# Dense 64-row chunks for the first stage of a maxout network, repacked by DMA, so that both products run as concurrent 64-row TensorE tiles

## Chip, cores, metric

One NeuronCore of a Trainium2 chip. The metric is the device time of the kernel in microseconds, median of several runs.

## The reference, cut to what matters

```python
# x (8, 4160, 192); weight (8 heads, 7 taps)
w = softmax(weight, axis=-1)
y[b, s, h, g] = sum_k w[h, k] * x_pad[b, s + k, h, g]      # causal, head = 24 channels
h = maximum(maximum(y @ w1, y @ w2), y @ w3)               # 192 -> 768
out = h @ w_out                                            # 768 -> 192, 33280 rows, fp32
```

The kernels use max(a, b, c) = max(a-c, b-c, 0) + c: the first stage computes y(w1-w3) and y(w2-w3), a relu and a maximum, and the second stage adds yM with M = w3 w_out.

## The kernel before

Rows come in 65 blocks of 512. The convolution is a matmul with a band matrix, one 32-column tile per head, so a head of 24 channels lies in a slot of 32 PSUM rows, and 192 channels take two halves of 128 rows.

```python
for (wsrc, q) in ...:                                   # weights padded the same way (cut)
    for half in range(2):
        for (s0, c0, cnt) in slot_rows(half):           # 24 rows each
            q.dma_start(out=st[s0:s0 + cnt, half, :], in_=wsrc[c0:c0 + cnt, :])

def conv(t):                                            # 40 matmuls, four column tiles at once
    ...
    for i in range(2):
        nc.scalar.copy(out=y[:, i, 0:N], in_=G[i][:, 0:N])

def l1(t, j):                                           # one 128-column group of the 768
    for i in range(2):                                  # the two products
        for half in range(2):
            nc.tensor.matmul(ps[i], lhsT=wd[i][:, half, P*j:P*(j+1)], rhs=y[:, half, :],
                             start=(half == 0), stop=(half == 1))
    nc.scalar.activation(out=r, in_=ps[0], func=AF.Relu)
    nc.vector.tensor_max(out=hs[t][:, j, :], in0=r, in1=ps[1])

for t in range(NB + 1):                                 # cut
    load_x(t + 3); cast_x(t + 2)                        # SyncE queue; GpSimd
    l1(t, 0); conv(t + 1); l1(t, 1)
    for j in range(2, NJ): st2(t - 1, j - 2); l1(t, j)
    store(t - 1)                                        # SyncE queue
```

## Time and profile before

| | before |
|---|---|
| time, median of 4 runs | 598.8 us |
| TensorE / VectorE / ScalarE / GpSimd busy | 94 / 57 / 50 / 12% |
| share of TensorE in the chain that ended last | 94% |
| one block | 8.50 us |
| mean granted TensorE clock | 0.997 |

The chain of work that ended last is the view to start from. It follows, back from the last instruction, what released each step. Where one engine holds nearly all of it, only shorter work on that engine helps; where it changes hands in a fixed pattern, the pattern is a loop, and its terms can be added up. The lines are in the prediction.

### The profile page before, as it was taken

How to read it: one execution, taken by the hardware profiler on the slowest of the kernel's cores; microseconds unless marked ns; L12 is line 12 of the kernel's file. 1: busy time of each engine (PE TensorE's matmuls, PEld its weight loads, DVE VectorE, ACT ScalarE, POOL GpSimd, SP SyncE). 2: the span in 40 equal slices, each digit the busy share in tenths (PEclk: the TensorE clock that was granted, in tenths of full speed). 3: DMA queues.
4: the chain of work that ended last, by engine and by line, in shares of the span. 5: the costliest groups of instructions: out<-in, count | busy, mean ns of one | idle time of the engine just before them, and what ended most of it. 6: DMA issues, size and time to landing. Idle time of an engine off the chain costs nothing.

```text
span 597.4 us, 15039 instructions
## 1 busy us (share of the span) xinstructions
PE 562.2 (94%) x6300; PEld 361.1 (60%) x6300; DVE 342.9 (57%) x542; ACT 299.2 (50%) x523; POOL 72.0 (12%) x95
## 2 busy tenths in 40 slices
PE   0199999999999999999999999999999999999995
PEld 0066666666666666666666666666666666666663
DVE  1645656555655565556555656565555656565663
ACT  1135555555555555555555555555555555555551
POOL 2200111101111011101101111011101110111100
PEclk9999999999999999999999999999999999999998
DMA  7502432333234323442344334323443343324211
GB/s 206 172 1 61 119 109 83 109 120 112 83 105 120 114 87 100 121 118 83 98 121 120 86 94 120 120 87 92 121 121 89 91 119 112 103 86 118 83 55 53
DMA packets 79107, 61.40 MB, mean 103 GB/s; under 512 B 2912, under 2 KB 78208, under 8 KB 79040
## 3 DMA queue, kind: packets, MB, share of 16 engines
q1 hardware_dynamic: 78032, 58.43, 33.3%
q10 hardware_dynamic: 1008, 2.02, 1.0%
q8 instruction: 49, 0.80, 0.6%
q14 instruction: 18, 0.15, 0.1%
HBM read 34.34 MB, written 26.09 MB: 101 GB/s over the span
## 4 chain that ended last, share of the span: by engine, by line
PE 94%; DMA 3%; DVE 1%; ACT 1%; ACTq 0%; issue 0%; SPq 0%
PE l L238 58%; PE pso L256 22%; PE pso L253 7%; PE G L221 6%; DMA xf<-in_x_dram 1%; PE pm L204 1%; DMA ws<-in_moe_w_dram 1%; DMA wk<-in_weight_dram 1%; DMA Rd<-R 1%; ACTq L170 0%; DVE h L242 0%; DVE ws L167 0%; ACT r L241 0%; ACT wo L189 0%; SPq L116 0%
## 5 line engine op out<-in xcount | busy, mean ns | idle before, releaser
L238 PE MATMUL l<-y,wd 128*128 128x512 f16 x1560 | 392.4, 381 | 9.0 <-ACT y L228 9.0
L242 DVE TENSOR_TENSOR h<-r,l 128x512 f16<-128x512 f16 x390 | 268.2, 688 | 224.8 <-ACT r L241 220.4
L241 ACT ACTIVATE r<-l 128x512 f16<-128x512 f32 x390 | 234.1, 600 | 235.2 <-PE l L238 235.2
L238 PEld LDWEIGHTS <-wd 128*128 128x128 f16 x1560 | 143.8, 98 | 121.2 <-DVE wd L186 9.6
L256 PE MATMUL pso<-wo,h 128*128 128x192 f16 x1560 | 171.4, 246 | 0.4 <-DVE h L242 0.4
L256 PEld LDWEIGHTS <-h 128*128 128x128 f16 x1560 | 132.7, 98 | 0.6 <-DVE h L242 0.6
L127 POOL CAST x<-xf 128x960 f16<-128x960 f32 (+3 forms) x88 | 70.0, 800 | 487.3 <-DMA xf<-in_x_dram 358.0
L253 PEld LDWEIGHTS <-y 128*128 128x128 f16 x520 | 50.8, 98 | 60.7
L253 PE MATMUL pso<-m,y 128*128 128x192 f16 x520 | 85.4, 246 | 0.0
L228 ACT CAST y<-G 128x512 f16<-128x512 f32 x130 | 69.8, 589 | 28.0 <-PE G L221 28.0
L259 DVE COPY o<-pso 128x384 f32<-128x384 f32 x130 | 71.6, 551 | 1.8 <-PE pso L256 1.8
L221 PEld LDWEIGHTS <-x 128*32 128x32 f16 (+2 forms) x2624 | 36.6, 98 | 45.5 <-issue 40.0
L221 PE MATMUL G<-band,x 128*32 128x122 f16 (+3 forms) x2624 | 43.1, 211 | 18.4 <-DVE band L154 18.4
L189 ACT CAST wo<-wos 128x1152 f16<-128x1152 f32 x1 | 1.2, 1152 | 21.6 <-DMA ws<-in_moe_w_dram 21.6
L154 DVE COPY band<-bandc 128x1072 f16<-128x1072 f16 x1 | 2.5, 2530 | 9.5 <-DMA bandc<-Rd 9.5
L186 DVE TENSOR_TENSOR wd<-ws,ws 128x768 f16<-128x768 f32 x4 | 3.8, 959 | 4.2 <-DMA ws<-in_moe_w_dram 4.2
L204 PE MATMUL pm<-wos,w3t 128*128 128x192 f32 x24 | 4.2, 330 | 0.0
L204 PEld LDWEIGHTS pm<-wos,w3t 128*128 128x128 f32 x24 | 3.9, 190 | 0.2 <-DVE w3t L199 0.2
L167 DVE MEMSET ws<- 128x1536 f32 x2 | 2.7, 1338 | 0.5 <-issue 0.3
L206 DVE CAST m<-pm 128x192 f16<-128x192 f32 x2 | 0.7, 357 | 3.1 <-PE pm L204 3.1
L198 PE MATMUL pt<-ident,ws 128*128 128x128 f32 x12 | 1.7, 277 | 0.7 <-DVE w3t L199 0.7
L141 DVE TENSOR_REDUCE wsum<-wexp 128x8 f32<-128x56 f32 x1 | 0.3, 251 | 3.2 <-ACT wexp L139 3.2
(14 smaller groups left out, 8.9 us busy)
## 6 DMA issues: line engine op xcount, KB each, us to landing
out_dram<-o SPq DMA_DIRECT2D x64, 384.0 KB
xf<-in_x_dram SPq DMA_DIRECT2D x48, 480.0 KB
xf<-in_x_dram SPq DMA_DIRECT2D x16, 384.0 KB
ws<-in_moe_w_dram ACTq DMA_DIRECT2D x16, 72.0 KB
xf<-in_x_dram SPq DMA_DIRECT2D x8, 96.0 KB
ws<-in_moe_w_dram SPq DMA_DIRECT2D x8, 72.0 KB
wos<-in_moe_w_out_dram SPq DMA_DIRECT2D x1, 576.0 KB
xf<-in_x_dram SPq DMA_DIRECT2D x8, 70.5 KB
```

Of the source, the lines that this page charges most:

```text
L127: nc.gpsimd.tensor_copy(out=x16[0:rl, q0:q1, :], in_=xf[0:rl, q0:q1, :])
L167: eng.memset(st[:], 0.0)
L186: nc.vector.tensor_sub(out=d16[:, half, :], in0=wa[:, half, :], in1=w3s[:, half, :])
L204: nc.tensor.matmul(ps[:], lhsT=w3t[:, j, half, :], rhs=wos[:, j, :], start=(j == 0), stop=(j == NJ - 1))
L221: nc.tensor.matmul(G[h // 4][32 * g:32 * g + 32, lo:hi], lhsT=x16[0:rlen, q, cb:cb + 32], rhs=band[0:rlen, h, cc:cc + hi - lo], start=True ...
L228: nc.scalar.copy(out=y[:, i, 0:N], in_=G[i][:, 0:N])
L238: nc.tensor.matmul(ps[i][:, 0:N], lhsT=wd[i][:, half, P * j:P * (j + 1)], rhs=y[:, half, 0:N], start=(half == 0), stop=(half == 1))
L241: nc.scalar.activation(out=r[:, 0:N], in_=ps[0][:, 0:N], func=AF.Relu)
L242: nc.vector.tensor_max(out=hs[t][:, j, 0:N], in0=r[:, 0:N], in1=ps[1][:, 0:N])
L253: nc.tensor.matmul(ps[:, s % 2, :], lhsT=y[:, half, sl], rhs=m16[:, half, :], start=(half == 0), stop=False)
L256: nc.tensor.matmul(ps[:, s % 2, :], lhsT=hT[:, j, sl], rhs=wo[:, j, :], start=False, stop=(j == NJ - 1))
L259: nc.vector.tensor_copy(out=outs[t][0][:, s - 1:s + 1, :], in_=ps[:])
```

## The change

The intent: 192 channels are three chunks of 64 rows, not two of 128. Packed densely, each product takes three 64-row passes, and the two products can stand in the upper and the lower 64 rows of the array at once: three pair-passes for four passes. For this the convolution's output is copied by DMA from the 32-row slots to dense 64-row chunks, once into rows 0 to 63 and once into rows 64 to 127.

```diff
+    for h in range(NHEAD):                       # ten pieces of 24, 16 or 8 rows
+        s0 = 32 * (h % 4) + (8 if h == NHEAD - 1 else 0)
+        ch = GRP * h
+        while ch < GRP * (h + 1):
+            n = min(GRP * (h + 1), HALF * (ch // HALF + 1)) - ch
+            pieces.append((h // 4, s0 + ch - GRP * h, ch // HALF, ch % HALF, n))
+            ch += n
+    def repack(t0, t1):                          # one or two blocks
+        for (half, s0, c, r0, n) in pieces:
+            for lo in (0, HALF):
+                nc.sync.dma_start(out=dense[v][lo + r0:lo + r0 + n, c, t],
+                                  in_=slots[v][s0:s0 + n, half, t])
-    def l1(t, j): ...
+    def session(t, u):                           # two 128-column groups
+        for j in (j0, j1):
+            for c in range(NC):                  # three chunks
+                for i in range(2):               # two row tiles
+                    row = slice(HALF * i, HALF * (i + 1))
+                    nc.tensor.matmul(ps[i, j], lhsT=wd[row, c, P * j:P * (j + 1)],
+                                     rhs=y[row, c, k:k + N], start=(c == 0), stop=(c == NC - 1))
...
+    conv(0); repack(0, 0); conv(1); repack(1, 1); make_m(); conv(2)
+    for t in range(NB):
+        load_x(t + 4); cast_x(t + 3)
+        session(t, 0)
+        conv(t + 3)
+        if t % 2 == 0:
+            repack(t + 2, t + 3)
+        session(t, 1); st2(t - 1, 0); session(t, 2); st2(t - 1, 2)
+        store(t - 1)
```

Cut: the band matrix is built from a zeroed DRAM tile and a small transfer of taps, weights come in four 64-row transfers, M is built from 64-row transposes, and the PSUM banks are shared out anew (two and three for the products, one for the second stage).

More of the change, by code (lines that the diff above doesn't have):

```diff
@@ L87 @@
     x16p = ctx.enter_context(tc.tile_pool(name="x16p", bufs=3))
-    yp = ctx.enter_context(tc.tile_pool(name="yp", bufs=3))
-    rp = ctx.enter_context(tc.tile_pool(name="rp", bufs=3))
+    ysp = ctx.enter_context(tc.tile_pool(name="ysp", bufs=3))
+    ydp = ctx.enter_context(tc.tile_pool(name="ydp", bufs=3))
+    rp = ctx.enter_context(tc.tile_pool(name="rp", bufs=4))
     hp = ctx.enter_context(tc.tile_pool(name="hp", bufs=2))
@@ L93 @@
     psg = ctx.enter_context(tc.tile_pool(name="psg", bufs=1, space=bass.MemoryType.PSUM))
-    psl = ctx.enter_context(tc.tile_pool(name="psl", bufs=2, space=bass.MemoryType.PSUM))
-    pst = ctx.enter_context(tc.tile_pool(name="pst", bufs=2, space=bass.MemoryType.PSUM))
+    psp = ctx.enter_context(tc.tile_pool(name="psp", bufs=2, space=bass.MemoryType.PSUM))
+    psq = ctx.enter_context(tc.tile_pool(name="psq", bufs=3, space=bass.MemoryType.PSUM))
+    pst = ctx.enter_context(tc.tile_pool(name="pst", bufs=1, space=bass.MemoryType.PSUM))
     xin = {}
@@ L128, in cast_x @@
         xin[t][1] = x16
+    BW = BAND_W * NHEAD
     wk = const.tile([P, NHEAD, KW], FP32)
@@ L135 @@
     load_x(0)
-    R = const.tile([P, RLEN, NHEAD], FP16)
-    nc.vector.memset(R[:], 0.0)
+    zero = const.tile([P, BW], FP16)
+    nc.vector.memset(zero[:], 0.0)
+    Rd = dram.tile([P, BW], FP16)
+    nc.scalar.dma_start(out=Rd[:], in_=zero[:])
     wexp = const.tile([P, KW, NHEAD], FP32)
@@ L143 @@
     nc.vector.reciprocal(out=wrec[:], in_=wsum[:])
+    taps = const.tile([P, KW, NHEAD], FP16)
     for k in range(KW):
-        nc.vector.tensor_mul(out=R[:, P - 1 + KW - 1 - k, :], in0=wexp[:, k, :], in1=wrec[:])
-    Rd = dram.tile([P, RLEN * NHEAD], FP16)
-    nc.scalar.dma_start(out=Rd[:], in_=R[:].rearrange("p u h -> p (u h)"))
-    bandc = const.tile([P, BAND_W, NHEAD], FP16)
-    nc.scalar.dma_start(
-        out=bandc[:].rearrange("p c h -> p (c h)"),
-        in_=bass.AP(tensor=Rd[:].tensor, offset=Rd[:].offset + (P - 1) * NHEAD,
-                    ap=[[(RLEN - 1) * NHEAD, P], [1, BAND_W * NHEAD]]))
-    band = const.tile([P, NHEAD, BAND_W], FP16)
-    nc.vector.tensor_copy(out=band[:].rearrange("p h c -> p c h"), in_=bandc[:])
-    def slot_rows(half):
-        if half == 0:
-            return [(32 * g, GRP * g, GRP) for g in range(4)]
-        return [(32 * g, 96 + GRP * g, GRP) for g in range(3)] + [(104, 168, GRP)]
-    ws = []
-    for i, (wsrc, eng, q) in enumerate(((moe_w1, nc.vector, nc.scalar),
-                                        (moe_w3, nc.gpsimd, nc.sync),
-                                        (moe_w2, nc.vector, nc.scalar))):
-        st = const.tile([P, 2, DFF], FP32, tag=f"ws{i}", name=f"ws{i}")
-        eng.memset(st[:], 0.0)
-        for half in range(2):
-            for (s0, c0, cnt) in slot_rows(half):
-                q.dma_start(out=st[s0:s0 + cnt, half, :], in_=wsrc[c0:c0 + cnt, :])
-        ws.append(st)
-    w1s, w3s, w2s = ws
+        nc.vector.tensor_mul(out=taps[:, KW - 1 - k, :], in0=wexp[:, k, :], in1=wrec[:])
+    nc.scalar.dma_start(
+        out=bass.AP(tensor=Rd[:].tensor, offset=Rd[:].offset,
+                    ap=[[BW + NHEAD, P], [1, KW * NHEAD]]),
+        in_=taps[:].rearrange("p k h -> p (k h)"))
+    bandc = const.tile([P, BAND_W, NHEAD], FP16)
+    nc.scalar.dma_start(out=bandc[:].rearrange("p c h -> p (c h)"), in_=Rd[:])
+    HALF, NC = 64, D // 64
+    ws = const.tile([P, NC, DFF], FP32)
+    w3s = const.tile([P, NC, DFF], FP32)
+    for (lo, st, wsrc) in ((0, ws, moe_w1), (0, w3s, moe_w3), (HALF, ws, moe_w2), (HALF, w3s, moe_w3)):
+        nc.sync.dma_start(out=st[lo:lo + HALF, :, :], in_=wsrc.rearrange("(c r) f -> r c f", r=HALF))
     wos = const.tile([P, NJ, D], FP32)
@@ L176 @@
     load_x(2)
+    load_x(3)
     cast_x(0)
@@ L179 @@
     make_identity(nc, ident[:])
+    w3t = const.tile([P, NJ, 2 * P], FP32)
+    nc.gpsimd.memset(w3t[:], 0.0)
     cast_x(1)
-    wd = []
-    for i, wa in enumerate((w1s, w2s)):
-        d16 = const.tile([P, 2, DFF], FP16, tag=f"wd{i}", name=f"wd{i}")
-        for half in range(2):
-            nc.vector.tensor_sub(out=d16[:, half, :], in0=wa[:, half, :], in1=w3s[:, half, :])
-        wd.append(d16)
+    cast_x(2)
+    wd = const.tile([P, NC, DFF], FP16)
+    for c in range(NC):
+        nc.vector.tensor_sub(out=wd[:, c, :], in0=ws[:, c, :], in1=w3s[:, c, :])
@@ L188 @@
+    band = const.tile([P, NHEAD, BAND_W], FP16)
+    hh = NHEAD // 2
+    nc.vector.tensor_copy(out=band[:, 0:hh, :].rearrange("p h c -> p c h"), in_=bandc[:, :, 0:hh])
+    nc.scalar.copy(out=band[:, hh:NHEAD, :].rearrange("p h c -> p c h"), in_=bandc[:, :, hh:NHEAD])
     wo = const.tile([P, NJ, D], FP16)
-    nc.scalar.copy(out=wo[:], in_=wos[:])
     m16 = const.tile([P, 2, D], FP16)
     def make_m():
-        w3t = const.tile([P, NJ, 2, P], FP32)
+        nc.scalar.copy(out=wo[:], in_=wos[:])
@@ L194, in make_m @@
         for g in range(NJ // 2):
-            ps = pst.tile([P, 4, P], FP32, tag="pso", name=f"pt{g}")
-            for k in range(4):
-                j, half = 2 * g + k // 2, k % 2
-                nc.tensor.transpose(ps[:, k, :], w3s[:, half, P * j:P * (j + 1)], ident[:])
-            nc.vector.tensor_copy(out=w3t[:, 2 * g:2 * g + 2, :, :].rearrange("p j a s -> p (j a) s"),
-                                  in_=ps[:])
+            ps = psq.tile([P, 2, D], FP32, tag="q", name=f"pt{g}")
+            for k in range(2):
+                js = slice(P * (2 * g + k), P * (2 * g + k + 1))
+                for c in range(NC):
+                    nc.tensor.transpose(ps[:, k, HALF * c:HALF * (c + 1)], w3s[0:HALF, c, js],
+                                        ident[0:HALF, 0:HALF])
@@ L201, in make_m @@
+            to = w3t[:, 2 * g:2 * g + 2, :]
+            nh = NHEAD - 1
+            nc.vector.tensor_copy(
+                out=to[:, :, 0:32 * nh].rearrange("p j (h s) -> p j h s", s=32)[:, :, :, 0:GRP],
+                in_=ps[:, :, 0:GRP * nh].rearrange("p j (h s) -> p j h s", s=GRP))
+            nc.vector.tensor_copy(out=to[:, :, 2 * P - GRP:2 * P], in_=ps[:, :, D - GRP:D])
         for half in range(2):
-            ps = pst.tile([P, D], FP32, tag="pso", name=f"pm{half}")
+            ps = psp.tile([P, D], FP32, tag="p", name=f"pm{half}")
@@ L203, in make_m @@
             for j in range(NJ):
-                nc.tensor.matmul(ps[:], lhsT=w3t[:, j, half, :], rhs=wos[:, j, :],
+                nc.tensor.matmul(ps[:], lhsT=w3t[:, j, P * half:P * (half + 1)], rhs=wos[:, j, :],
                                  start=(j == 0), stop=(j == NJ - 1))
             nc.vector.tensor_copy(out=m16[:, half, :], in_=ps[:])
-    ys, hs, outs = {}, {}, {}
+    slots, dense, hs, outs = {}, {}, {}, {}
     def conv(t):
@@ L225, in conv @@
                     start=True, stop=True, tile_position=(0, 32 * g))
-        y = yp.tile([P, 2, NBLK], FP16, tag="y", name=f"y_{t}")
+        v, k = t // 2, t % 2
+        if k == 0:
+            slots[v] = ysp.tile([P, 2, 2 * NBLK], FP16, tag="ys", name=f"ys_{v}")
         for i in range(2):
-            nc.scalar.copy(out=y[:, i, 0:N], in_=G[i][:, 0:N])
-        ys[t] = y
+            nc.scalar.copy(out=slots[v][:, i, NBLK * k:NBLK * k + N], in_=G[i][:, 0:N])
         xin.pop(t)
-    def l1(t, j):
-        N = blkN[t]
-        y = ys[t]
-        ps = [psl.tile([P, NBLK], FP32, tag=f"l{i}", name=f"l{i}_{t}_{j}") for i in range(2)]
-        for i in range(2):
-            for half in range(2):
-                nc.tensor.matmul(ps[i][:, 0:N], lhsT=wd[i][:, half, P * j:P * (j + 1)],
-                                 rhs=y[:, half, 0:N], start=(half == 0), stop=(half == 1))
-        r = rp.tile([P, NBLK], FP16, tag="r", name=f"r_{t}_{j}")
-        nc.scalar.activation(out=r[:, 0:N], in_=ps[0][:, 0:N], func=AF.Relu)
-        nc.vector.tensor_max(out=hs[t][:, j, 0:N], in0=r[:, 0:N], in1=ps[1][:, 0:N])
@@ L244, in st2 @@
-    def st2(t, s):
+    pieces = []
+    for h in range(NHEAD):
[6 more added lines that the diff above has]
+    def repack(t0, t1):
+        if t0 >= NB:
+            return
+        t1 = min(t1, NB - 1)
+        v = t0 // 2
+        if t0 % 2 == 0:
+            dense[v] = ydp.tile([P, NC, 2 * NBLK], FP16, tag="yd", name=f"yd_{v}")
+        t = slice(NBLK * (t0 % 2), NBLK * (t1 % 2 + 1))
+        for (half, s0, c, r0, n) in pieces:
+            for lo in (0, HALF):
+                nc.sync.dma_start(out=dense[v][lo + r0:lo + r0 + n, c, t],
+                                  in_=slots[v][s0:s0 + n, half, t])
@@ new lines, in session @@
+    def session(t, u):
+        N, k = blkN[t], NBLK * (t % 2)
+        y = dense[t // 2]
+        j0, j1 = 2 * u, 2 * u + 1
+        ps = {(i, j): (psp, psq)[i].tile([P, NBLK], FP32, tag="pq"[i], name=f"l{i}_{t}_{j}")
+              for j in (j0, j1) for i in range(2)}
+        for j in (j0, j1):
+            for c in range(NC):
+                for i in range(2):
+                    row = slice(HALF * i, HALF * (i + 1))
+                    nc.tensor.matmul(ps[i, j][:, 0:N], lhsT=wd[row, c, P * j:P * (j + 1)],
+                                     rhs=y[row, c, k:k + N], start=(c == 0), stop=(c == NC - 1))
+        for j in (j0, j1):
+            r = rp.tile([P, NBLK], FP16, tag="r", name=f"r_{t}_{j}")
+            nc.scalar.activation(out=r[:, 0:N], in_=ps[0, j][:, 0:N], func=AF.Relu)
+            nc.vector.tensor_max(out=hs[t][:, j, 0:N], in0=r[:, 0:N], in1=ps[1, j][:, 0:N])
@@ L245, in st2 @@
+    def st2(t, s0):
         if t < 0:
             return
-        y, hT = ys[t], hs[t]
-        sl = slice(P * s, P * (s + 1))
-        if s % 2 == 0:
-            outs[t][1] = pst.tile([P, 2, D], FP32, tag="pso", name=f"pso_{t}_{s}")
-        ps = outs[t][1]
-        for half in range(2):
-            nc.tensor.matmul(ps[:, s % 2, :], lhsT=y[:, half, sl], rhs=m16[:, half, :],
-                             start=(half == 0), stop=False)
-        for j in range(NJ):
-            nc.tensor.matmul(ps[:, s % 2, :], lhsT=hT[:, j, sl], rhs=wo[:, j, :],
-                             start=False, stop=(j == NJ - 1))
@@ L258, in st2 @@
-        if s % 2 == 1:
-            nc.vector.tensor_copy(out=outs[t][0][:, s - 1:s + 1, :], in_=ps[:])
+        hT, ys = hs[t], slots[t // 2]
+        ps = pst.tile([P, 2, D], FP32, tag="o", name=f"po_{t}_{s0}")
+        for s in (s0, s0 + 1):
+            k = NBLK * (t % 2) + P * s
+            for i in range(2):
+                nc.tensor.matmul(ps[:, s % 2, :], lhsT=ys[:, i, k:k + P], rhs=m16[:, i, :],
+                                 start=(i == 0), stop=False)
+            for j in range(NJ):
+                nc.tensor.matmul(ps[:, s % 2, :], lhsT=hT[:, j, P * s:P * (s + 1)],
+                                 rhs=wo[:, j, :], start=False, stop=(j == NJ - 1))
@@ L261, in store @@
+        nc.vector.tensor_copy(out=outs[t][:, s0:s0 + 2, :], in_=ps[:])
     def store(t):
@@ L263, in store @@
             return
-        ob = outs.pop(t)[0]
+        ob = outs.pop(t)
         for (b, S, n, off) in blocks[t]:
@@ L273, in store @@
                 nc.sync.dma_start(out=out[g0:g0 + n, :], in_=ob[p0:p0 + n, s, :])
-        ys.pop(t)
         hs.pop(t)
@@ L278 @@
     conv(0)
-    for t in range(NB + 1):
-        if t < NB:
-            load_x(t + 3)
-            cast_x(t + 2)
-            hs[t] = hp.tile([P, NJ, NBLK], FP16, tag="h", name=f"h_{t}")
-            outs[t] = [outp.tile([P, 4, D], FP32, tag="o", name=f"o_{t}"), None]
-            l1(t, 0)
-            conv(t + 1)
-            l1(t, 1)
-            for j in range(2, NJ):
-                st2(t - 1, j - 2)
-                l1(t, j)
-            if t == 0:
-                make_m()
-        else:
-            for s in range(4):
-                st2(t - 1, s)
+    repack(0, 0)
+    conv(1)
+    repack(1, 1)
+    make_m()
+    conv(2)
+    for t in range(NB):
+        load_x(t + 4)
+        cast_x(t + 3)
+        hs[t] = hp.tile([P, NJ, NBLK], FP16, tag="h", name=f"h_{t}")
+        outs[t] = outp.tile([P, 4, D], FP32, tag="o", name=f"o_{t}")
+        session(t, 0)
+        conv(t + 3)
+        if t % 2 == 0:
+            repack(t + 2, t + 3)
+        session(t, 1)
+        st2(t - 1, 0)
+        session(t, 2)
+        st2(t - 1, 2)
         store(t - 1)
+    st2(NB - 1, 0)
+    st2(NB - 1, 2)
+    store(NB - 1)
 _INS = ['x', 'weight', 'moe_w1', 'moe_w2', 'moe_w3', 'moe_w_out']
```

## The prediction

> **What bounds the kernel now.** I read the page first: busy shares, then the chain that ended last, then the groups. Then I read the chain piece by piece for one block, and the queue that issues transfers.
>
> ```profile
> span 597.4 us, 15039 instructions
> PE 562.2 (94%) x6300; PEld 361.1 (60%) x6300; DVE 342.9 (57%) x542; ACT 299.2 (50%) x523; POOL 72.0 (12%) x95
> ...
> PE l L238 58%; PE pso L256 22%; PE pso L253 7%; PE G L221 6%; DMA xf<-in_x_dram 1%; PE pm L204 1%; DMA ws<-in_moe_w_dram 1%; DMA wk<-in_weight_dram 1%; DMA Rd<-R 1%; ACTq L170 0%; DVE h L242 0%; DVE ws L167 0%; ACT r L241 0%; ACT wo L189 0%
> ...
> L238 PE MATMUL l<-y,wd 128*128 128x512 f16 x1560 | 392.4, 381 | 9.0 <-ACT y L228 9.0
> ```
>
> TensorE carries 94% of the chain, and the first-stage product (L238) 58% of the span. Its waits are 9.0 us in all, so shorter TensorE work shows in the end until something else binds. The chain in order of time shows one block's pieces:
>
> ```profile
> 561.63 1.73 PE l L238 x8
> 563.36 0.58 PE G L221 x40
> 563.94 0.97 PE l L238 x4
> 564.91 0.17 PE pso L253 x2
> 565.08 0.49 PE pso L256 x6
> 565.57 0.86 PE l L238 x4
> ```
>
> Eight first-stage products take 1.73 us, so 0.216 us each (the 381 ns of the group row includes pipeline latency). The four after the convolution take 0.97, 0.11 more. A block is 24 first-stage products (1.73+0.97+3x0.86 = 5.28 us), four second-stage slices (4x0.66 = 2.64) and the convolution (0.58): 8.50 us. Successive stores on the SyncE queue are also 8.50 apart:
>
> ```profile
> 60.52 0.38 SPq L268 DMA_DIRECT2D out_dram<-o  x1
> 61.00 0.45 SPq L116 DMA_DIRECT2D xf<-in_x_dram  x1
> 69.02 0.38 SPq L268 DMA_DIRECT2D out_dram<-o  x1
> ...
> 95.01 0.46 SPq L116 DMA_DIRECT2D xf<-in_x_dram  x1
> ...
> 99.88 0.99 POOL L127 CAST x<-xf 128x960 f16<-128x960 f32 x1 [8.05 <-DMA xf<-in_x_dram]
> ...
> 22.10 0.80 ACTq L170 DMA_DIRECT2D ws<-in_moe_w_dram  x2
> 22.52 0.80 ACTq L170 DMA_DIRECT2D ws<-in_moe_w_dram  x2
> ```
>
> Three things to see. The issuing queue is nearly empty now: one store and one load in 8.5 us. A 480 KB load issued at 95.01 is cast at 99.88, 4.9 us later; other blocks give 4.3 to 5.6, so I take 4.7. And an issue costs the queue about the same whatever its size: the 24-row weight pieces start 0.42 us apart, as 384 and 480 KB transfers hold it 0.38 and 0.46. The 24-row pieces landed about 2.4 us after their issue (the fourth, issued at 21.27, let the subtraction start at 23.86).
>
> **What the Trainium skill says.** "TensorEngine Tiling (Array Packing)", Key Properties: tiles work independently, but changing the tiling mode drains TensorE. The trace agrees on both: 40 convolution products in four column tiles take 0.58 us, 14.5 ns each, where 122 columns at the first stage's rate would take 51 ns (0.216/512x122); and the first products after a mode change cost 0.11 more. Row tiles are not in this trace. "TensorE: Matmul & The Clock Gate", Part 3, Measured speedup vs the span model, gives about 4 ns for each extra tile, so a pair of 64-row products should cost nearly one. "DMA: Bandwidth & Descriptors", Rules for kernel authors, says that many small transfers should be merged and that under 64 KB one mostly pays overhead; the 0.42 us between issues agrees.
>
> **The change part by part.**
>
> *First stage.* 192 channels sit in two padded 128-row halves, so each product of one 128-column group costs two passes, four for both products. Dense 64-row chunks make three passes per product, with the two products side by side: three pair-passes for four passes. 18 pairs x 0.216 = 3.89 us per block instead of 24 x 0.216 = 5.18. Saved: 1.29 us per block, 84 us over 65 blocks.
>
> *Mode changes.* Convolution (column tiles), first stage (row tiles), second stage (whole array) now alternate six times per block, where it was two. The old two cost 0.11+0.05 (0.58 less 40x13.3 ns). Six at 0.05 to 0.11: about 0.5 in all, 0.35 more than before. TensorE per block: 3.89+2.64+0.53+0.5 = 7.6. The second-stage output has one PSUM bank now instead of two, so the second slice pair waits for the first's VectorE copy (0.55 us, queued behind two 0.69 us maxima): 0.1 to 0.3 more. TensorE alone: 7.7 to 7.9 per block, 15.4 to 15.8 per two blocks.
>
> *Repack.* Heads of 24 rows against chunks of 64 give ten pieces (heads 2 and 5 are cut), each sent twice: 20 transfers for every two blocks, all on SyncE. At 0.415 us each: 8.3 us of issue per pair, beside 2 stores and 2 loads (1.9). The queue is 10.2 us busy of some 16: not full, but in strict order, and that makes a loop. In the program the order is: repack of blocks t+2,t+3; store t-1; load t+5. The load of t+5 is what the convolution of t+5 needs two blocks later, and the next repack needs that convolution. Once round, per two blocks:
> - 20 issues 8.3
> - store issue 0.48
> - load from issue to cast 4.7
> - cast 0.99
> - first convolution product to the end of both ScalarE copies 1.77 (308.10 to 309.87 in the trace)
> - semaphores between them, some 0.3.
> Sum 16.5 us, 8.27 per block. It exceeds TensorE's 15.4 to 15.8, so I expect TensorE to stand 0.7 to 1.1 us per pair before every second convolution, waiting for a cast. The other loop (repack landing 2.4 after its last issue, then a session 1.4, then the convolution) is 0.1+8.3+2.4+1.4+1.77 = 14.0 and hides.
>
> *Bytes.* 192 rows x 2 copies x 2 KB = 0.79 MB per pair, 26 MB over the run on top of 61. The 16 DMA engines are 33% busy with the present 58 MB, so about 48% after. No bound.
>
> *Other engines.* The relu, maximum and copy counts do not change: VectorE 6x0.688+2x0.551 = 5.23 us per block and ScalarE 6x0.600+2x0.589 = 4.78. Both stay under 8.27.
>
> *Beginning.* First stage now starts at 28.4 us. After: the band copy stands behind the three subtractions that need all weights, so the first convolution comes near 21 to 22 us (estimate: bandc landed at 15.8; three subtractions at 0.96 and a 1.3 us half copy). Its copies end at 24.5, the first repack's issues at 33, its landing at 35. The second repack is issued until 41, the third until 50, and the loop's first load only then: convolution 5 near 56. Building M (6.4 us of TensorE, exposed now at 36.9 to 43.3) goes under the first repack.
>
> *Sum.* Convolution 5 at 56; 29 pairs to convolution 63 at 16.5 = 478; after it the rest of that block (5.8), four blocks at 7.8 (31), the last second stage (2.7), and 6.8 from TensorE's end to the end of the span as now: 580. The measured time is 1.7 above the span: **582 us**. I take **580**, allowing a little for a load that lands sooner.
>
> **The rivals.**
> - *TensorE stays the bound.* If the issues come at 0.35 us (the shortest rows are 0.30), the loop is 15.2 and hidden: 65x7.8 = 507 plus some 40 at both ends, about 547. For it: issues after a wait were 0.30 to 0.31. Against: 16 in a row averaged 0.415.
> - *The issuing queue binds harder.* Waits on unrelated transfers exist (a load of x waited 1.5 us for Rd<-R), and the repack competes with stores and loads. At 0.45 per issue or a load of 5.6, the loop is about 17.3: 23 us more, about 605, no gain left.
> - *Row tiles overlap badly.* Each pair needs two weight loads of 98 ns in 216 ns; if they are not hidden, a pair costs 0.28 us, a first stage 5.0, a block 8.9: 65x8.9+40 = 618. Against: the convolution's tiles overlap almost wholly.
> - *Slower beginning.* If block 0's products wait for both early repacks, 5 to 6 us more.
>
> **Range and chances.** The gain of 84 us from TensorE is nearly sure in kind; what is left depends on 20 issues' length and one load's latency, each moving the total by 20 to 30 us. So 545 to 610, a wide range. Faster by over 2% means below 587: 0.62. Within 2%: 0.28. Slower: 0.10, mostly the third rival.
>
> **What would show it.** Right: pairs of first-stage products 0.216 us apart; 20 repack issues in a row of about 8.3 us on SyncE per two blocks; stores unevenly spaced, 16.5 us per two; TensorE idle before every second convolution, released by POOL's cast. TensorE's share of the span should fall to about 85 to 90%. Wrong: no idle before the convolution (the first rival), waits of the first stage on dense tiles (repack landing late), or pairs clearly slower than 0.216. What I know least is whether the load really ends last in that loop.

## The result, and the profile after

| | before | changed |
|---|---|---|
| time, median of 4 runs | 598.8 us | 810.63 us |
| ratio, 95% interval | | 1.353 (1.350 to 1.357) |
| TensorE in the chain | 94% | 39% |
| mean granted TensorE clock | 0.997 | 0.868 |

A ratio is the mean time of one kernel's fast runs over that of the other's fast runs of the same rounds, so it is not quite the ratio of the medians. The prediction was wrong: 580 us, range 545 to 610.

The page of the changed kernel: span and busy times, the granted clock in 40 slices, and the chain by line.

```profile
span 807.6 us, 17651 instructions
PE 594.3 (74%) x7086; PEld 341.1 (42%) x7086; DVE 340.4 (42%) x542; ACT 301.8 (37%) x524; POOL 70.7 (9%) x95
...
PEclk9977988898898978899979888998888899988899
...
SPq L257 24%; PE l L272 21%; DMA xf<-in_x_dram 20%; PE po L290 9%; PE G L224 4%; PE po L287 4%; POOL x L129 3%; SPq L301 2%; ACT r L276 1%; DMA Rd<-taps 1%; DMA bandc<-Rd 1%; ACT ys L233 1%; DMA yd<-ys 1%; DMA Rd<-zero 1%; DVE o L292 1%
```

TensorE no longer bounds. The largest entry is SPq L257: time in which SyncE's queue issues the repack, that is, starts its transfers one after the other. After it in the loop come the load of x (20%) and the cast. In order of time the chain shows the loop (start, duration, what; one turn, with like rows left out):

```profile
336.19 1.00 POOL x L129
337.23 1.07 PE G L224 x40
338.40 0.40 issue
338.80 0.60 ACT ys L233
...
339.73 0.73 SPq L257
340.52 0.71 SPq L257
...
352.74 0.71 SPq L257
353.56 0.46 SPq L301
354.12 4.75 DMA xf<-in_x_dram
359.01 1.00 POOL x L129
```

Cast, convolution, ScalarE copy, twenty issues, store, load, and the next cast: the loop of the prediction, closed in the order it gave. But each issue takes 0.73 us, not 0.415. This is one of 6 bursts of 33 in which the chain stays on the queue. In the others it crosses over to the products that run beside the burst, at an issue that ScalarE released last; from there comes most of TensorE's 39%. Yet the queue waited there for 8.8 us in the whole run (17 times, never over 0.8 us), and, read from the queue and the engines themselves, the loop closes in nearly every turn. The queue itself over one turn (start, duration, merged rows of one kind):

```profile
338.93 14.52 SPq L257 DMA_DIRECT2D yd<-ys  x20
353.56 0.46 SPq L301 DMA_DIRECT2D out_dram<-o  x1
354.12 0.44 SPq L118 DMA_DIRECT2D xf<-in_x_dram  x1
...
361.75 14.90 SPq L257 DMA_DIRECT2D yd<-ys  x20
```

From one repack to the next 22.8 us pass; the mean between 80 and 680 us is 23.5, against 16.5 predicted and 17.0 for two blocks before. TensorE's idle time, by who ended it (total us, times, longest):

```profile
PE G L224 <- POOL x L129: 127.8, 39, 5.7
...
PE l L272 <- DMA yd<-ys: 51.4, 62, 3.3
```

The convolution waits for the cast, as predicted, and for longer. Two sessions of twelve first-stage products and the convolution after such a wait:

```profile
408.14 1.05 PE L224 MATMUL G<-band,x 128*32 128x122 f16 x40 [5.23 <-POOL x L129]
...
409.12 2.74 PE L272 MATMUL l<-yd,wd 64*128 64x512 f16 x12
...
419.13 1.47 PE L272 MATMUL l<-yd,wd 64*128 64x512 f16 x12
```

The first session after a 5 us stop takes nearly twice as long as a later one. The granted clock of this core was 0.58 on the mean during the stop (403.0 to 408.1), 0.50 from 408.1 to 413.0 and 1.00 from 414.3 on. This agrees with the Trainium skill, "TensorE: Matmul & The Clock Gate", Part 1, by which an idle window of about 3.4 us lowers the clock. It is a consequence of the stops: e2 and e5 below, without them, have a granted clock of 0.992 and 0.994.

### The profile page after: what moved, and what is told of

It is laid out like the page before. It is cut to its first block, busy times and chain, and to the rows that moved or that the text cites. A ratio compares the mean times of both kernels' runs of the same rounds, so it can differ in the third digit from the quotient of the medians.

```text
span 807.6 us, 17651 instructions
## 1 busy us (share of the span) xinstructions
PE 594.3 (74%) x7086; PEld 341.1 (42%) x7086; DVE 340.4 (42%) x542; ACT 301.8 (37%) x524; POOL 70.7 (9%) x95
## 4 chain that ended last, share of the span: by engine, by line
PE 39%; SPq 26%; DMA 23%; issue 3%; POOL 3%; ACT 2%; DVE 1%; POOLq 0%; ACTq 0%
SPq L257 24%; PE l L272 21%; DMA xf<-in_x_dram 20%; PE po L290 9%; PE G L224 4%; PE po L287 4%; POOL x L129 3%; SPq L301 2%; ACT r L276 1%; DMA Rd<-taps 1%; DMA bandc<-Rd 1%; ACT ys L233 1%; DMA yd<-ys 1%; DMA Rd<-zero 1%; DVE o L292 1%
## 5 line engine op out<-in xcount | busy, mean ns | idle before, releaser
L272 PE MATMUL l<-yd,wd 64*128 64x512 f16 x2340 | 345.5, 418 | 52.0 <-DMA yd<-ys 51.4
L272 PEld LDWEIGHTS <-wd 64*128 64x128 f16 x2340 | 108.9, 101 | 206.2 <-issue 114.4
L290 PE MATMUL po<-wo,h 128*128 128x192 f16 x1560 | 180.4, 254 | 0.0
L224 PE MATMUL G<-band,x 128*32 128x122 f16 (+3 forms) x2624 | 57.5, 247 | 154.1 <-POOL x L129 127.8
L290 PEld LDWEIGHTS <-h 128*128 128x128 f16 x1560 | 140.7, 102 | 1.7
L233 ACT CAST ys<-G 128x512 f16<-128x512 f32 x130 | 69.8, 589 | 159.5 <-PE G L224 159.3
L224 PEld LDWEIGHTS <-x 128*32 128x32 f16 (+2 forms) x2624 | 48.6, 118 | 186.0 <-POOL x L129 151.0
L287 PE MATMUL po<-m,ys 128*128 128x192 f16 x520 | 91.6, 260 | 1.3 <-DVE o L292 1.3
L292 DVE COPY o<-po 128x384 f32<-128x384 f32 x130 | 72.5, 558 | 26.9 <-PE po L290 18.1
L287 PEld LDWEIGHTS <-ys 128*128 128x128 f16 x520 | 40.1, 101 | 66.4 <-issue 66.1
```

Of the source, the lines that this page charges most:

```text
L224: nc.tensor.matmul(G[h // 4][32 * g:32 * g + 32, lo:hi], lhsT=x16[0:rlen, q, cb:cb + 32], rhs=band[0:rlen, h, cc:cc + hi - lo], start=True ...
L233: nc.scalar.copy(out=slots[v][:, i, NBLK * k:NBLK * k + N], in_=G[i][:, 0:N])
L272: nc.tensor.matmul(ps[i, j][:, 0:N], lhsT=wd[row, c, P * j:P * (j + 1)], rhs=y[row, c, k:k + N], start=(c == 0), stop=(c == NC - 1))
L287: nc.tensor.matmul(ps[:, s % 2, :], lhsT=ys[:, i, k:k + P], rhs=m16[:, i, :], start=(i == 0), stop=False)
L290: nc.tensor.matmul(ps[:, s % 2, :], lhsT=hT[:, j, P * s:P * (s + 1)], rhs=wo[:, j, :], start=False, stop=(j == NJ - 1))
L292: nc.vector.tensor_copy(out=outs[t][:, s0:s0 + 2, :], in_=ps[:])
```

## The experiments

Eleven kernels ran. The kernel before was run beside each of them (medians 598.7, 599.1 and 599.0 us). "Period" is the mean distance from the start of one repack to that of the next, between 80 and 680 us of the span, that is, the time of two blocks.

| run | time, us | ratio to before | period, us |
|---|---|---|---|
| changed kernel | 811 | 1.353 | 23.5 |
| e1, loads ahead | 704 | 1.177 | 19.8 |
| e2, one copy (wrong result) | 558 | 0.932 | 15.4 |
| e3, convolution ahead too | 680 | 1.135 | 18.9 |
| e5, through DRAM, loads ahead | 550.5 | 0.920 | 15.4 |
| e6, 20 transfers, source in DRAM | 672 | 1.121 | 19.0 |
| e7, four more in the loop | 911 | 1.521 | 26.7 |
| e8, four more in the gap | 828 | 1.382 | 23.7 |
| e10, one copy, then a copy of it | 586 | 0.980 | 16.3 |
| e11, through DRAM alone | 587 | 0.979 | 16.4 |

The theory for all of them: the order of the SyncE queue closes a loop, and the length of 20 issues sets it. The rivals: the repack's bytes slow the DMA engines, or the row tiles and the lower clock cost the time.

**e1: only the loads earlier.**

```diff
-    xfp bufs=4            +    xfp bufs=6
-        load_x(t + 4)     +        load_x(t + 6)       # and load_x(4), load_x(5) ahead of the loop
```

> Edit: only the loads of x are issued two blocks earlier (two more input buffers), so that none that a near convolution needs stands behind a repack in the SyncE queue. Theory (the queue's strict order closes a loop: 20 repack issues 14.6 us, store, load 4.9 us, cast, convolution, copy = 22.8 us per two blocks): that loop opens, and the next one binds: first copy of the convolution to the last repack landed (14.6 + 2.1), the rest of a session (0.9), the convolution up to its first copy (1.7) = about 19 us per two blocks. Time about 680 us, POOL idle for loads no longer at the head of the waits, TensorE now waiting for dense tiles before the even blocks. Rival A (the repack traffic slows the DMA engines, the loads simply land late): no more than 2% gained, about 800. Rival B (64-row pairs or the lowered TensorE clock cost the time): unchanged at 810.

Measured 704 us, 24 over what I expected, period 19.8. Taking the load out of the loop is worth 106 us with every transfer and product still there, so neither rival carries this half of the loss. The next loop is where the theory put it, 0.8 longer: the burst of 20 issues grew to 15.3 us on average, now that loads and stores are in flight beside it.

**e2: one of the two copies.**

```diff
-            for lo in (0, HALF):
+            for lo in (0,):
-    rhs=y[row, c, k:k + N]
+    rhs=(y, yhi)[i][row, c, k:k + N]      # yhi: zeros; result wrong on purpose
```

> Edit: only the lower copy of the dense tile is repacked (10 transfers per two blocks instead of 20); the upper half is a constant tile of zeros, so the result is wrong on purpose. TensorE's work is the same. Theory: the loop falls by 10 issues of 0.73 to about 15.5 us per two blocks, which is TensorE's own 15.3; time about 550 us, granted clock back near 1.0. Rival A (DMA contention): half of the repack bytes, so about half of the 211 us lost, 700. Rival B (row tiles or clock): 800, since every product is still there.

Measured 558 us, granted clock 0.992. The commonest period is 15.27 us, TensorE's own time for two blocks (also the median of e5). All products are there, so row tiles and mode changes cost nothing that was not predicted. This run also shows the pairs, since the two tiles read different tensors (timeline: start, duration, instruction):

```profile
290.88 0.39 PE L274 MATMUL l<-yd,wd 64*128 64x512 f16 x1
290.88 0.39 PE L274 MATMUL l<-yhi,wd 64*128 64x512 f16 x1
...
291.10 0.38 PE L274 MATMUL l<-yd,wd 64*128 64x512 f16 x1
291.11 0.38 PE L274 MATMUL l<-yhi,wd 64*128 64x512 f16 x1
```

The two products start within 0.01 us of each other and the next pair 0.22 us later: two 64-row products in the time of one.

**e3: convolution and repack two blocks earlier as well.**

```diff
-        load_x(t + 4); cast_x(t + 3)      +        load_x(t + 7); cast_x(t + 5)
-        conv(t + 3)                       +        conv(t + 5)
-            repack(t + 2, t + 3)          +            repack(t + 4, t + 5)
                                           # one more slot buffer; loads 4 to 6, conv(3), repack(2, 3), conv(4) ahead of the loop
```

> Edit: loads three blocks earlier, and convolution and repack two blocks earlier (one more slot buffer); work and transfers unchanged. Theory: both loops open, and what is left is the SyncE queue's sum, 20 issues 14.6 + two stores and two loads 2.6 = 17.2 us per two blocks: about 620 us, the queue busy without a gap. Rival (latency of landing, not issue, limits): no better than the run with only the loads ahead, about 680.

Measured 680 us: 60 over what I expected, and the very number that I had given the rival, so the time alone does not decide. The queue does (start, duration):

```profile
338.43 14.87 SPq L260 DMA_DIRECT2D yd<-ys  x20
353.40 0.46 SPq L304 DMA_DIRECT2D out_dram<-o  x1
...
355.37 0.63 SPq L118 DMA_DIRECT2D xf<-in_x_dram  x1
356.09 16.05 SPq L260 DMA_DIRECT2D yd<-ys  x20
```

It issues without a gap: bursts of 15.55 us on average and 2.83 us of stores and loads, 18.4 of a period of 18.9; the rest is the 0.1 us between one kind and the next. The loops are open and the queue's sum is the bound, as the theory said; what I had too small was again the issues, 0.78 us from one to the next with other transfers in flight (0.73 expected).

**e4: the length of an issue by itself.** The kernel before with, for instance:

```diff
+    for i in range(6):
+        nc.sync.dma_start(out=dst[64:88, i, 0:2048], in_=src[32:56, 0:2, :]...)   # 24 rows x 4 KB, SBUF to SBUF
+    for i in range(6):
+        nc.sync.dma_start(out=dst[24:48, i, 0:1024], in_=dsd[i, 0:24, 0:1024])    # 24 rows x 2 KB, DRAM to SBUF
```

> The kernel before, with six transfers in a row of each of twelve forms added at its end; results unchanged. Read: the time an issue holds its queue. Theory 1 (the form costs it: both ends in SBUF): 24 rows x 2 KB from SBUF to SBUF about 0.72 us, the same rows from DRAM to SBUF or from SBUF to DRAM 0.3 to 0.4, whatever the bytes. Theory 2 (a row costs it, number of rows or bytes): 1 KB and 4 KB rows differ, and DRAM forms are as long as SBUF ones. Theory 3 (a queue already full slows each further issue): the first of six is short in every form, the later ones long.

The issues of four forms (shortest/median/longest in ns): 24 rows of 1 KB and of 4 KB within SBUF, 24 rows of 2 KB from DRAM to SBUF, and from SBUF to DRAM.

```profile
L308 SPq DMA_DIRECT2D dst<-src x6: 713/714/714, 607.2 to 611.0; - x6
...
L310 SPq DMA_DIRECT2D dst<-src x6: 713/714/714, 611.8 to 615.5; - x6
...
L318 SPq DMA_DIRECT2D dst<-dsd x6: 331/362/568, 628.3 to 630.7; - x6
...
L320 SPq DMA_DIRECT2D dsq<-src x6: 289/338/531, 631.1 to 635.3; - x6
```

An issue of 24 rows within SBUF, the form of 12 of the repack's 20 issues, takes 0.714 us whatever its bytes, twice that of the same rows with one end in DRAM. The other forms of e4 (medians): 16, 8 and 128 rows within SBUF 0.59, 0.63 and 0.60 us; 64x3 rows 1.57 within SBUF (0.50 to 1.92) and 0.59 from DRAM; the 24 rows issued from ScalarE's queue 0.73 and from GpSimd 0.51. So it was not the queue that made the weights' 0.415, which were issued from ScalarE, shorter. It is the form, not the bytes, and not a queue that fills up: the 1 KB and 4 KB rows above vary by 1 ns over six in a row. Theory 3 is nevertheless true elsewhere: the same 24 rows of 2 KB, sent straight after six transfers of 768 KB, took 1.32 us (median).

**e9: which part of the form.** Ten more forms in the same way.

> The kernel before with six transfers each of ten forms at its end: 24 rows between the same partitions, to other partitions, 32 rows, 64 rows, one row, 24 rows of fp32, DRAM to SBUF, DRAM to DRAM, SBUF to DRAM with 32 rows. If both ends in SBUF are what costs, all six SBUF forms hold the queue 0.5 us or more, and all forms with an end in DRAM 0.3 to 0.4, DRAM to DRAM included. If moving rows to other partitions costs it, the form between the same partitions is short (0.35). If the number of rows costs it, one row is short and 64 rows long.

| 2 KB rows (median issue, us) | |
|---|---|
| SBUF to SBUF, 24 rows, other or same partitions, fp16 or fp32 | 0.71 |
| SBUF to SBUF, 1, 32 or 64 rows | 0.59, 0.59, 0.60 |
| DRAM to SBUF, 24 rows | 0.36 |
| SBUF to DRAM, 32 rows | 0.43 |
| DRAM to DRAM, 24 rows | 0.59 |

```profile
L309 SPq DMA_DIRECT2D dst<-src x6: 713/714/880, 597.1 to 601.1; - x6
...
L323 SPq DMA_DIRECT2D dsq<-dsd x6: 554/587/589, 625.6 to 628.7; - x6
```

Moving to other partitions does not cost it (L309 stays on the same ones), nor does the number of rows. One expectation failed: DRAM to DRAM (L323) is long as well. So it is not SBUF at both ends; in the forms of 24 and 32 rows tried, both ends in the same memory are long (0.59 to 0.71), and one of each is short (0.34 to 0.43). Why, and why 24 rows cost 0.12 more than 1, 32 or 64, no run here tells.

**e6: the same 20 destinations, source in DRAM.**

```diff
+        for half in range(2):
+            nc.sync.dma_start(out=dr[half, :, t], in_=slots[v][:, half, t])
-                                  in_=slots[v][s0:s0 + n, half, t])
+                                  in_=dr[half, s0:s0 + n, t])
```

> Edit: the changed kernel with the same 20 transfers into the dense tile, same rows and same order of the queue, but their source is a DRAM copy of the padded slots, written by two more transfers. Theory (both ends in SBUF make an issue long): 20 issues of 0.38 to 0.40 = 7.8 us, two writes 0.9 and a landing of about 3 in front of them; loop 0.9+0.5+3+7.8+0.6+4.9+1+1.7 = 20.4 us per two blocks against 23.4: about 715 us although there are two transfers and one landing more. Rival (the number of transfers counts, whatever their ends): 22 issues of 0.73 and the landing, 27 us, 920.

Measured 672 us, period 19.0. Two transfers and a landing more, and yet 139 us less than the changed kernel: 20 issues took 8.3 us on average in place of 14.9. The rival that counts transfers is dead. It came out below 715 because the landing was shorter than the 3 us I gave it (the first read stands 2.6 us after the first write, where the loop had 0.9+0.5+3) and because I had left out the beginning, where three bursts follow each other.

**e7 and e8: four more transfers, in the loop or in the gap.**

```diff
+    def extra():                       # 24 rows x 2 KB to a scratch tile
+        for i in range(4):
+            nc.sync.dma_start(out=scr[64:88, i, :], in_=zsrc[0:24, :])
             repack(t + 2, t + 3)
+            extra()                    # e7; in e8 it stands ahead of repack
```

> Edit: the changed kernel with four more 24-row transfers from SBUF to SBUF (a scratch tile) behind every repack, ahead of the store and the next load. Theory: four issues of 0.73 to 0.77 join the loop, +3.0 us per two blocks, +96 us: 905. Rival (the loop is not set by issue time but by landing of data or by TensorE): no change, 810 to 820.

> Edit: the same four transfers, but ahead of the repack and behind the load, where the queue stands waiting some 6 us for the convolution's copy. Theory: they are hidden, 805 to 820. Rival (more transfers cost wherever they stand, by DMA load or by the queue's total): +96 us as in the run before, or a good part of it.

Measured 911 us (+100) and 828 us (+17). The queue in e7, then in e8:

```profile
337.74 2.99 SPq L266 DMA_DIRECT2D scr<-zsrc  x4
```

```profile
314.27 3.43 SPq L266 DMA_DIRECT2D scr<-zsrc  x4
319.73 14.57 SPq L257 DMA_DIRECT2D yd<-ys  x20
```

The same work costs 100 us where it lengthens the loop and 17 where the queue stood waiting, so place decides. The 17 us are 8 above my limit. The traces tell where they arise: of 20.6 us between the two profiled spans, 3.8 come before the loop's second turn and 10.2 at the end, over the last two repacks, where no gap hid the four (the last but one began 4.0 us after the copies that it needs). Only 6.6 come in the 28 turns between, 0.2 us each. The loads were not slower: from issue to cast 4.9 us on the mean, 5.0 in the changed kernel. For the rival no more than the 0.2 us a turn speaks.

**e5: through DRAM, loads ahead.** Eight writes make a dense DRAM tile, two reads fill both halves.

```diff
-        for (half, s0, c, r0, n) in pieces: ... (20 transfers)
+        for h in range(NHEAD):
+            nc.sync.dma_start(out=dr[GRP*h:GRP*(h+1), t], in_=slots[v][s0:s0+GRP, h//4, t])
+        for lo in (0, HALF):
+            nc.sync.dma_start(out=dense[v][lo:lo + HALF, :, t],
+                              in_=dr[:, t].rearrange("(c r) f -> r c f", r=HALF))
```

> Edit: the dense tile is made through DRAM: eight 24-row writes from the slots and two 64x3-row reads for every two blocks (10 issues in place of 20, none with both ends in SBUF), loads two blocks earlier. Theory: a write issue is 0.30 to 0.34 us, a read 0.6, so 4 us of issue instead of 14.6; the first copy to the dense tile landed is some 10 us, both loops are under TensorE's 15.3 us per two blocks, and TensorE is the bound: 550 us (540 to 560), 8% faster than the kernel before. Rival (the way through DRAM lands too late, or the added traffic delays loads): TensorE waits for dense tiles, 580 to 640.

Measured 550.5 us, 8% faster than the kernel before, and correct. The queue and the chain by engine:

```profile
318.13 4.21 SPq L261 DMA_DIRECT2D dr<-ys  x8
324.72 1.24 SPq L263 DMA_DIRECT2D yd<-dr  x2
```

```profile
PE 86%; DMA 10%; SPq 2%; ACT 1%; DVE 0%; issue 0%; ACTq 0%
```

TensorE is the bound again, with 100 MB moved in place of 87: more bytes and less time. The DMA queue's share of the 16 engines rose to 65% and did no harm.

**e10 and e11: the parts of it.**

```diff
# e10: ten pieces into the lower rows, then one transfer; loads ahead
+        nc.sync.dma_start(out=dense[v][HALF:P, :, t], in_=dense[v][0:HALF, :, t])
# e11: e5 with loads in the old place
-        load_x(t + 6)
+        load_x(t + 4)
```

> Edit: the lower copy is repacked piece by piece as in the changed kernel (10 issues), the upper one is a single 64x3-row transfer from the lower when that has landed; loads two blocks earlier. Theory: 7.3 us of issue, 1.4 of waiting for the landing, 0.5 for the copy and some 3 for its landing; the loop over the dense tile is 1.7+6.6+2.1+3+0.9 = 14.3 us per two blocks, the queue's sum 12: both under TensorE's 15.3, so 550 to 565, although everything stays in SBUF. Rival (transfers within SBUF are slow as such): over 600.

> Edit: the way through DRAM alone, loads in the old place behind the repack. Theory: the loop over the load is 5.9 (writes and their landing) + 1.2 (reads) + 0.6 + 5.5 (load) + 1 + 1.7 = 15.9 us per two blocks, just over TensorE's 15.3: about 570 us, so nearly all of the gain comes from the shorter issues. Rival (the earlier loads made the gain): 650 or more.

Measured 586 and 587 us, periods 16.3 and 16.4: both about 2% below the kernel before, but the intervals of their ratios (0.977 to 0.982 and 0.974 to 0.984) reach across the 2% limit, so the verdict is unclear. Both missed what I expected (550 to 565, about 570). In e11 the loop over the load is 0.5 longer than reckoned and runs at the load's pace. In this order the fewer and shorter issues give 224 of the 260 us and the earlier loads the last 36; taken first, the loads gave 106 (e1). In e10 TensorE waited 23 us for the upper copy. From the start of that copy's issue to the product that waited for it 4.15 us passed (median of 22), where the loop had 3; with 0.6 more before it, that makes 16.1 of the period of 16.3.

## Why the prediction was wrong, point by point

- **TensorE's saving: right.** Pairs 0.22 us apart; two blocks without a stop take 15.3 us, predicted 15.4 to 15.8. The wait for the one PSUM bank of the second stage (0.1 to 0.3 a block) did not come: 1.3 us in the whole run, of the changed kernel as of e2.
- **Mode changes: right in size.** A block without a stop is 7.64 us (half of the 15.27 us in e2); products at their rates are 3.89+2.64+0.53 = 7.06, leaving about 0.1 for each of six changes.
- **The loop: right in kind and order.** It binds, TensorE waits for POOL's cast, and e1, e7 and e8 show that work counts by its place in the loop.
- **Its first term, "20 issues 8.3": wrong, and this is the step that failed.** Measured 14.6 from the first issue to the store behind it. The others of that turn were close (over all turns between 80 and 680 us the load took 5.0 on the mean):

| term | predicted | measured |
|---|---|---|
| 20 issues | 8.3 | 14.63 |
| store issue | 0.48 | 0.56 |
| load, issue to cast | 4.7 | 4.89 |
| cast, and to the convolution | 0.99 (+0.3 semaphores, all) | 1.04 |
| convolution to the first repack | 1.77 | 1.70 |
| sum | 16.5 | 22.82 |

The agreement of 1.77 and 1.70 is luck: the 1.77 was a convolution of 0.58 and both ScalarE copies, but the repack starts after the first copy, and the convolution took 1.07 at the lowered clock. The two errors cancel.

I had taken 0.415 us from 24-row transfers of weights, DRAM to SBUF, and applied it to transfers from SBUF to SBUF, of which the kernel before has none. No line of its profile could have given the number; a range of issue lengths should have covered that. My rival "the issuing queue binds harder" went only to 0.45, the same form with some contention. My chance of 0.10 for slower lay mostly on the row tiles, which were not slow (pairs 0.22 us apart).
- **A misreading without effect.** The landing of 2.4 us is 2.6 by the line's own numbers (21.27 to 23.86); that loop stays hidden either way. The rival's 0.28 us for a pair follows from no number shown.
- **The sum.** Convolution 5 was put at 56 us and came at 78.3: three bursts at the beginning, 6.6 us longer each, are 20 of the 22; the rest is the first burst's start, 27.3 for 24.5. The 29 pairs took 677.6 us instead of 478. The rest took 51.7 instead of 46. Together 807.6, the span.
- **Bytes: right.** No run shows the DMA engines as the bound.
- **Not foreseen: the clock.** Stops of some 5 us lower it; the loop pays for it in the convolution, 1.07 us instead of about 0.6 in the turn shown.

## What to carry to other kernels

Count the issues of a queue as work of an engine, in strict order, and draw what stands behind them: a load behind a long burst joins a loop that no utilization figure shows. Measure the issue in the very form that will be used, its two ends included, before trusting a figure from another form. A longer way with fewer and shorter issues (through DRAM: 10 in place of 20, 13 MB more) can beat the direct one.

## What the Trainium skill lacked or had wrong

- "DMA: Bandwidth & Descriptors": its section Issuing engines are not separate DMA queues calls the sequencer's time for initiating a DMA usually small relative to the DMA itself. One issue is: 0.73 us, where the last transfer of a repack let its product start 2.2 us after its issue began. But here 20 issues in a row were the largest part of a 22.8 us loop, and fewer and shorter ones were worth 224 us (e11 against the changed kernel). Its rules warn of many small transfers (no run here tests the limit of 64 KB that the prediction took from them), and a table compares the sequencer's time for one DMA on older and newer chips, but no length of an issue is given by its two ends. Measured for 24 rows: 0.71 us SBUF to SBUF, 0.59 DRAM to DRAM, 0.36 DRAM to SBUF, 0.34 SBUF to DRAM, the first independent of bytes (1 to 4 KB a row); and 0.73 and 0.51 SBUF to SBUF when ScalarE and GpSimd issue it.
- "TensorEngine Tiling (Array Packing)", Key Properties: it says that a change of mode drains TensorE, without a size. Here about 0.1 us for each change (0.58 us over six changes in a block of 7.64).
